# Attention over listed key blocks: tiles of 64 queries by three chunks of 128 keys, batch by batch over all heads

## The chip, the cores and the metric

The kernel runs on one core of one Trainium2 chip. The core has a tensor engine (PE; its weight loads are told apart as PEld), a vector engine (DVE), a scalar engine (ACT), GpSimd (POOL), a sync engine (SP) that mostly issues transfers, and 16 DMA engines that all queues share. Operands lie in on-chip memory of 128 partitions; the tensor engine writes its products into eight accumulation banks per partition.

The metric is the device time of one execution in microseconds. The kernel before took 692.69, 695.46 and 695.71 us in three runs: a median of 695.46 us.

## What is computed

Block-sparse attention, followed by a mixture of experts in which each token goes to one expert:

```python
# q, k, v: (4 batches, 8 heads, 768 positions, 64); blocks of 32, so 24 blocks
mask = |blk_i - blk_j| <= 1
mask |= (blk_i == 0) | (blk_j == 0) | (blk_i == 23) | (blk_j == 23)
for qb in range(24):
    for kb in sampled_blocks[qb]:            # 3 drawn blocks for each query block
        mask[qb*32:(qb+1)*32, kb*32:(kb+1)*32] = True
attn = softmax(where(mask, q @ k.T / 8, -1e9))
x = (attn @ v) with heads side by side       # (3072 tokens, 512)

logits = x @ w_gate                          # (3072, 8 experts)
expert = argmax(logits)
y = relu(x @ w1[expert]) @ w2[expert]        # 512 -> 1024 -> 512
return softmax(logits)[expert] * y
```

The drawn blocks are an input, so which keys a query sees is known only on the chip. An inner query block sees at most its own block and its two neighbours, the first and the last block, and three drawn ones. The first and the last query block see every key.

## The kernel before

Everything is float32; each float32 matmul shows in the trace as two weight loads and two matmuls.

**Attention** walks over 16 pairs `(b, pr)`: a batch and two heads, whose 64 dimensions fill the 128 partitions together. Each pair has two steps (`half`), for 384 of the 768 queries each, so 32 steps. `load` brings k, q and v of a pair on SP's queue, position p*6+c to partition p. `turn` transposes k and q by the tensor engine (12 transposes of 64x128) and ACT copies the result out. A step then makes six score units, one for each chunk c of 128 keys (`scores`): two products of 64x128 by 384 queries (line 244), one for each head, each on its half of the array's rows; an exp by ACT of the whole unit, 128x768 (line 249); and a product by DVE with a 0/1 mask (line 253). All keys are computed, and the mask removes those that are not listed. The mask for all 768x768 positions is built at the start (`make_mask`, `make_late`); the first step uses a penalty in the scores instead. `attend` multiplies the weights with v (line 265): for each chunk 12 products of 128 keys by 64 queries and 65 columns, the last column being ones, which gives the sum. Two such products stand side by side in the array, on 64 columns each.

After a step's last chunk, `divide` (DVE) takes sums, reciprocals and the product, and SP stores rows of x to DRAM in pieces of 512 bytes. One step later `turn_out` transposes x and ACT copies it, and `logits` multiplies it with the gate's weights. Logits are summed up over the four head pairs of a batch.

Scores, turned tiles and the mask's tables share a ring of three slots of accumulation memory (`ps_s`, two banks each); attention's products have one bank, x turned has one. The order of work on POOL, PE and DVE is the program's own, on ACT too in the loop of steps; the order on SP is left to the planner there.

**Routing and experts.** When three batches are done, phase A assigns their tokens to tiles of 128 tokens of one expert (`ranks`, `count`, `layout_a`, `slots_a`, `one_hots`, `tokens`), between attention steps of the last batch. Five such tiles are worked first; phase B places the rest while they run. Weights of an expert (2 MB for each of the two layers) are fetched by SP at an address read from a table; there are two buffers for each layer. Rows of x are gathered by POOL with an indirect DMA (`gather`), transposed, multiplied (`layer1`, line 815; `layer2`, line 829), and results are scattered to the output (`put`). Three larger and three small groups are worked among the tiles (`layers_u`, `layer1_s`, `layer2_s`).

At the end `judge` checks that all sums of exps and all logits lie in fixed bounds. If not, or if there are more tiles than foreseen, a switch runs more tiles or the whole of attention again with a maximum subtracted (`attention_again`).

Of the kernel before, what the change touches and what calls it, by code (L numbers as in the profile page):

```python
# [17 lines left out]
def kernel(  # L18
# [65 lines left out]
    ps_o = ctx.enter_context(tc.tile_pool(name="ps_o", bufs=1, space=PSUM))  # L84
    ps_x = ctx.enter_context(tc.tile_pool(name="ps_x", bufs=1, space=PSUM))
# [3 lines left out]
    def lend(to, **pools):  # L89
        to.close()  # L90
        for name, bufs in pools.items():
            upper[name] = to.enter_context(tc.tile_pool(name=name, bufs=bufs, space=PSUM, reuse_waits="tile"))

    lend(lent, ps_s=3)
    ld = ctx.enter_context(tc.tile_pool(name="ld", bufs=2))

    ea = mpool.tile([P, 8, NCH * P], F32, name="ea")

    def e_slot(n, half, c):
        return ea[:, ((2 * n + half) * NCH + c) % 8, :].rearrange("p (h q) -> p h q", h=2)  # L100

    HC = NCH // 2
    loaded, turned = {}, {}
    pairs = [(b, pr) for b in range(B) for pr in range(NPR)]
    NA = (B - 1) * NPR

    VW = D + 4
    values = [mpool.tile([P, 2, NCH, VW], F32, name=f"v_{j}") for j in range(3)]

    def load(b, pr):  # L110
        got = []
        for src, nm in ((k, "k_sb"), (q, "q_sb")):
            t = ld.tile([P, NCH, 2, D], F32, name=nm)
            for hh in range(2):
                nc.sync.dma_start(t[:, :, hh, :], src[b, 2 * pr + hh].rearrange("(p c) d -> p c d", p=P))
            got.append(t)
        t = values[pairs.index((b, pr)) % 3]
        for hh in range(2):
            nc.sync.dma_start(t[:, hh, :, :D], v[b, 2 * pr + hh].rearrange("(p c) d -> p c d", p=P))
        got.append(t)  # L120
        loaded[(b, pr)] = got


    oh = mpool.tile([P, NCH, P], BF16, name="oh")
    pen = mpool.tile([P, S], BF16, name="pen")
    assert NCH == 6
    mask = mpool.tile([P, NCH, S], BF16, name="mask")

    ones = mpool.tile([P, 1], F32, name="ones")

    sums = mpool.tile([P, 2 * B * NPR, 2 * HC], F32, name="sums")
    nc.vector.memset(ones[:], 1.0)

    def make_mask(pool):

        halves = bass.DRamTensorHandle(sampled_blocks.tensor.name, (2 * NB * NR,), I32)
# [823 lines left out]
    for which in range(2):  # L960
        turn(0, 0, which)
# [222 lines left out]
```

## Time and profile before

| | |
|---|---|
| three runs, median | 695.46 us (692.69 to 695.71) |
| profiled execution: its time / its span | 694.1 us / 692.4 us |
| first score product, first attention product | 8.65 us, 15.98 us |
| one step of attention | 9.69 us, constant from 31 to 263 us |
| last `divide` | 324.7 us |
| first expert matmul (line 815) | 325.9 us |
| from there to the end | 366.5 us |
| granted tensor clock, mean | 0.995 |

A line of the costliest groups names source line, engine, operation, what is written and read, the shape (a tensor operation's weights first, such as 128*64, then partitions x columns of the moving operand), and the count. Behind the first bar are busy microseconds and the mean nanoseconds of one; behind the second the engine's idle time ahead of them and what ended it. In the timeline a line starts with its start and its length. Matmuls overlap, so a mean of 223 ns for one says little; busy time over count is the pace.

### The profile page before, as it was taken

The page shows a single profiled execution, that of the slowest core. Times are in us where ns is not written, and L with a number is a line of the kernel's source. Part 1 is how long each engine was busy: PE and PEld are TensorE (multiplying, and loading weights), DVE is VectorE, ACT ScalarE, POOL GpSimd, SP SyncE. Part 2 cuts the span into 40 slices and gives each one's busy share as a digit, 9 for nine tenths or more (in the row PEclk, how much of TensorE's full clock was granted, in tenths as well). Part 3 has the DMA queues.
Part 4 walks back from the last instruction along what each step waited for, and adds up shares of the span by engine and source line. Part 5 has one row for each costly group of instructions (what it writes and reads, how often), then busy time and mean ns, then how long its engine had stood idle before and what let it go on. Part 6 is the DMA issues. An engine that isn't in the chain of part 4 may idle for free.

```text
span 692.4 us, 19727 instructions
## 1 busy us (share of the span) xinstructions
PE 671.0 (97%) x8586; PEld 511.7 (74%) x8586; DVE 340.5 (49%) x825; ACT 231.5 (33%) x393; POOL 66.2 (10%) x106
## 2 busy tenths in 40 slices
PE   8999999999999999998999999999999999999993
PEld 6777777777787777777867776696779778767861
DVE  6566766666666767885392059410254022702200
ACT  4555655566555664553211101112111111111110
POOL 4000000000000000003011221102120113010210
PEclk9999999999999999999999999999999999999998
DMA  9423443343323442853598999977996699989950
GB/s 190 102 64 86 94 93 86 81 94 93 77 60 78 93 94 50 332 204 88 171 317 303 307 340 383 343 278 259 402 397 235 239 387 393 358 274 390 396 173 18
DMA packets 135196, 145.78 MB, mean 211 GB/s; under 512 B 80995, under 2 KB 93283, under 8 KB 135076
## 3 DMA queue, kind: packets, MB, share of 16 engines
q1 hardware_dynamic: 130672, 130.15, 58.2%
q0 software_dynamic: 4368, 14.02, 5.3%
q8 instruction: 77, 1.26, 0.8%
q14 instruction: 43, 0.35, 0.2%
q10 hardware_dynamic: 36, 0.00, 0.0%
HBM read 131.47 MB, written 12.94 MB: 209 GB/s over the span
## 4 chain that ended last, share of the span: by engine, by line
PE 55%; issue 35%; POOL 4%; DVE 4%; POOLq 0%; another core or an unknown queue 0%; ACT 0%; DVEq 0%
PE op L265 20%; PE s L244 19%; PE hp L815 6%; PE zp L829 3%; PE tp L222 2%; PE xr L294 2%; POOL out_dram L844 2%; POOL xg L747 2%; PE xr L305 1%; PE idle L180 1%; DVE orB L677 1%; POOL ea L867 0%; POOL ea L912 0%; DVE tkB L697 0%; PE bm L195 0%
## 5 line engine op out<-in xcount | busy, mean ns | idle before, releaser
L253 DVE TENSOR_TENSOR ea<-ea,mask 128x768 f32<-128x768 f32 x186 | 164.3, 953 | 30.1 <-ACT ea L249 30.1
L265 PE MATMUL op<-v,ea 128*64 128x65 f32 x4608 | 148.4, 223 | 0.0
L815 PEld LDWEIGHTS hp<-xgT,w 128*128 128x128 f32 x1216 | 138.4, 192 | 8.9 <-issue 5.8
L265 PEld LDWEIGHTS op<-v,ea 128*64 128x64 f32 x4608 | 140.1, 138 | 5.9 <-DVE ea L253 4.4
L249 ACT ACTIVATE ea<-s 128x768 f32<-128x768 f32 x192 | 139.6, 851 | 13.8 <-PE s L244 10.8
L815 PE MATMUL hp<-xgT,w 128*128 128x128 f32 x1216 | 141.1, 276 | 2.7 <-ACT hT L822 1.4
L244 PE MATMUL s<-qT,kT 64*128 64x384 f32 x768 | 134.6, 495 | 0.8 <-DVE qT L228 0.8
L796 DVE STREAM_TRANSPOSE xgT<-xg 32x128 f32<-32x128 f32 x208 | 62.9, 303 | 128.9 <-PE hp L815 63.4
L829 PE MATMUL zp<-w,hT 128*128 128x512 f32 x256 | 112.7, 594 | 0.4 <-DMA w<-in_moe_w_dram 0.4
L244 PEld LDWEIGHTS s<-qT,kT 64*128 64x128 f32 x768 | 64.7, 186 | 51.2 <-ACT ea L249 32.5
L829 PEld LDWEIGHTS zp<-w,hT 128*128 128x128 f32 x256 | 47.6, 191 | 55.0 <-issue 54.3
L822 ACT ACTIVATE hT<-hp 128x512 f32<-128x512 f32 x36 | 21.5, 597 | 117.0 <-PE hp L815 98.6
L834 ACT ACTIVATE zo<-zp,xg 128x512 f32<-128x512 f32 x16 | 11.0, 687 | 101.3 <-PE zp L829 101.3
L922 DVE STREAM_TRANSPOSE ea<-ea 32x128 f32<-32x128 f32 x84 | 21.7, 285 | 30.1 <-DMA ea<-x_rows,gB 29.5
L747 POOL DMA_INDIRECT xg<-x_rows,gA x5 | 6.3, 1266 | 299.1 <-PE s L244 297.9
L230 ACT COPY kT<-tp 128x384 f32<-128x384 f32 x30 | 12.9, 482 | 63.4 <-PE tp L222 63.4
L230 ACT COPY qT<-tp 128x384 f32<-128x384 f32 x30 | 12.9, 483 | 61.4 <-PE tp L222 61.4
L844 POOL DMA_INDIRECT out_dram<-zo,sB x14 | 14.0, 1003 | 167.3 <-ACT zo L834 119.5
L313 DVE TENSOR_TENSOR lgn<-lgn,xr 128x24 f32<-128x24 f32 x24 | 4.3, 179 | 42.5 <-PE xr L305 42.5
L294 PEld LDWEIGHTS xr<-ident,xb 128*128 128x128 f32 x96 | 9.9, 140 | 16.9 <-DVE ea L253 15.3
L829 PE MATMUL hpu<-w,hT 128*128 128x512 f32 x48 | 21.1, 593 | 0.0
L933 PEld LDWEIGHTS hpu<-ea,w 128*128 128x128 f32 x96 | 15.2, 190 | 4.7 <-ACT zo L834 4.2
(279 smaller groups left out, 439.0 us busy)
## 6 DMA issues: line engine op xcount, KB each, us to landing
w<-in_moe_w_dram SPq DMA_DIRECT2D x50, 2048.0 KB, 10.8
k_sb<-in_k_dram SPq DMA_DIRECT2D x32, 192.0 KB, 4.2
q_sb<-in_q_dram SPq DMA_DIRECT2D x32, 192.0 KB, 3.3
v<-in_v_dram SPq DMA_DIRECT2D x32, 192.0 KB, 3.4
x_rows<-xb SPq DMA_DIRECT2D x16, 384.0 KB, 4.2
xg<-x_rows,gB POOLq DMA_INDIRECT x15
out_dram<-zo,sB POOLq DMA_INDIRECT x14
x_rows<-gw SPq DMA_DIRECT2D x4, 24.0 KB, 2.7
```

What stands on the lines that cost most here:

```text
L230: nc.scalar.copy(to[:, j], got[:, j])
L244: nc.tensor.matmul(s[:, hh, :CW], lhsT=kT[r, c * P : (c + 1) * P], rhs=qT[r, cols], start=True, stop=late)
L249: nc.scalar.activation(e, s[:, :, :CW], AF.Exp, scale=scale)
L253: nc.vector.tensor_tensor(e, e, m[:, None, :].to_broadcast([P, 2, CW]), op=ALU.mult)
L265: nc.tensor.matmul(op[j * D : (j + 1) * D, m, hh, : D + 1], lhsT=e[:, hh, m * P + j * D : m * P + (j + 1) * D], rhs=v_sb[:, hh, c, : D + 1 ...
L294: nc.tensor.transpose(xr[:, m * P : (m + 1) * P], xbs[n][:, half * HC + m, :], ident[:])
L796: nc.vector.transpose(xT[d, :, t], xg[t, :DM].rearrange("p (c q) -> p c q", c=DB)[:, :, d])
L815: nc.tensor.matmul(hp[:, m, :], lhsT=st[i]["w1"][:, c, fb * P : (fb + 1) * P], rhs=st[i]["xT"][:, c, :], start=(c == 0), stop=(c == DB - 1),)
L822: nc.scalar.activation(hT[:, g * (FB // 2) : (g + 1) * (FB // 2), :], hp[:], AF.Relu)
L829: nc.tensor.matmul(zp[:], lhsT=st[i]["hT"][:, fb, :], rhs=st[i]["w2"][:, fb, :], start=(fb == 0), stop=(fb == FB - 1),)
L844: ins = nc.gpsimd.indirect_dma_start(out=to[:, :], out_offset=bass.IndirectOffsetOnAxis(ap=at, axis=0), in_=rows, in_offset=None, bounds_c ...
L922: nc.vector.transpose(xT_u[d, :, j * P + tq * 32 : j * P + (tq + 1) * 32], xg_u[t, j, :DM].rearrange("p (c q) -> p c q", c=DB)[:, :, d],)
```

## The change

Attention is laid out anew; the experts' arithmetic stays.

**Tiles of queries.** The 22 inner query blocks make 11 tiles of 64 queries (two blocks each, tile t: blocks 2t+1 and 2t+2). Blocks 0 and 23 together are a twelfth. For each inner tile the keys are three chunks of 128: chunk 0 is the window, blocks 2t to 2t+3; chunk 1 is blocks 0 and 23 and two drawn blocks; chunk 2 is four drawn blocks. So 384 keys are computed for it instead of 768. A 0/1 mask per tile and chunk removes what a query does not see, drawn blocks that repeat or that the other chunks hold among it. The twelfth tile has all six chunks and no mask.

**Order.** The outermost loop is the batch, then a group g of two tiles (g = 5 first: the last inner tile and the end blocks; then 0 to 4), then two halves of two head pairs each: 48 steps. k and q of a whole batch, all heads, lie turned in one of two sets (`sets`); while a batch is worked, the next one's k and q are loaded (`fill_stage`), turned, and its v loaded.

**Scores.** A unit is again 128x768 and gets one exp and one mask product, but it is made of 24 products of 64 dimensions x 64 keys by 64 queries, one for each tile, chunk, head and half of a chunk, each on a 64x64 quarter of the array.

**Drawn blocks.** Keys: `place_keys` copies six blocks of 32 columns per tile, of all four head pairs at once (128x128), from the turned k to a buffer (`kr`), at addresses that ACT and DVE load into registers from a table; three on each, or all six on ACT for the last batch. Values: v of a batch is stored back to DRAM as rows of 520 numbers (all heads, each with its 1 for the sum; `keep_v`), and `fetch_values` gathers 128 such rows for each of chunks 1 and 2 with an indirect DMA on POOL, and the window that lies across two chunks with a plain one on SP.

**Around it.** x is stored as whole rows of 2048 bytes. Logits of 128 tokens are now summed over all heads in the accumulation memory. `turn_out` and phase A's small products use slots of the ring `ps_s`; attention's products have two banks. The order on ACT and SP is written out by hand too. The large mask and its tables go. The experts' buffers lie in memory that attention used (`room`, `around`, `kr`); two for each kind, as before. The twelfth tile of batch 0 is scored at the start, as each head pair arrives.

```diff
-    ps_o = ctx.enter_context(tc.tile_pool(name="ps_o", bufs=1, space=PSUM))
-    ps_x = ctx.enter_context(tc.tile_pool(name="ps_x", bufs=1, space=PSUM))
+    ps_o = ctx.enter_context(tc.tile_pool(name="ps_o", bufs=2, space=PSUM))
...
+    order = [GL] + list(range(GL))
+    VW = D + 1
+    VR = H * VW
+    NKR = 2 * NR * BLK
...
+    def load_v(b, hs=None):
+        for h in range(H) if hs is None else hs:
+            nc.sync.dma_start(sets[b][2][:, :, h * VW : h * VW + D], v[b, h].rearrange("(c p) d -> p c d", p=P))
+
+    def keep_v(b):
+        nc.sync.dma_start(v_d[b].rearrange("(c p) w -> p c w", p=P), sets[b][2])
...
+    def scores(items, m=None):
+
+        s = upper["ps_s"].tile([P, 2, 512], F32, name="s")
+        w = D * len(items)
+        for x, (keys, queries) in enumerate(items):
+            for hh in range(2):
+                r = slice(hh * D, (hh + 1) * D)
+                for j in range(2):
+                    nc.tensor.matmul(
+                        s[j * D : (j + 1) * D, hh, x * D : (x + 1) * D], lhsT=keys(r, j), rhs=queries(r), start=True, stop=True,
+                    )
+        e = ea[:, units[0] % 8, :].rearrange("p (h w) -> p h w", h=2)
+        units[0] += 1
+        nc.scalar.activation(e[:, :, :w], s[:, :, :w], AF.Exp, scale=scale)
+        return e
...
+    def unit(b, g, pr):
+        e = scores([(keys_of(b, g, pr, ti, ch), queries_of(b, g, pr, ti)) for ti in range(2) for ch in range(3)])
+        masked(e, g)
+        return e
...
+    def attend(b, g, pr, e):
+        for ch in range(3):
+            for hh in range(2):
+                for ti in range(2):
+                    x = 3 * ti + ch
+                    product(b, g, pr, ti, hh, e[:, hh, x * D : (x + 1) * D], values_of(b, g, ti, ch), ch == 2)
...
+    def fetch_values(b, g):
+        par = parity(b, g)
+        if g < GL:
+            row = D * (2 * g + 1)
+            nc.sync.dma_start(around[:, par, 0, :], v_d[b][row : row + P, :])
+        for ti, t in enumerate(tiles_of(g)):
+            for ch in range(2):
+                nc.gpsimd.indirect_dma_start(
+                    out=around[:, par, 1 + 2 * ti + ch, :], out_offset=None, in_=v_d[b][:, :],
+                    in_offset=bass.IndirectOffsetOnAxis(ap=rows_of[:, 2 * t + ch : 2 * t + ch + 1], axis=0),
+                )
+
+    def place_keys(b, g, ti, prs=slice(0, NPR), on_vector=NR):
+
+        t = tiles_of(g)[ti]
+        par = parity(b, g)
+        cut = 2 * NR - on_vector
+        for nm, a, z in (("Activation", 0, cut), ("DVE", cut, 2 * NR)):
+            if a == z:
+                continue
+            _, at = nc.values_load_multi_w_load_instructions(
+                from_k[0:1, NR + 2 * NR * t + a : NR + 2 * NR * t + z], engines=(getattr(mybir.EngineType, nm),),
+                min_val=0, max_val=S - BLK, skip_runtime_bounds_check_because="clamped on the chip to the blocks that there are",
+            )
+            for i, v_ in zip(range(a, z), at):
+                (nc.scalar.copy if nm == "Activation" else nc.vector.tensor_copy)(
+                    kr[:, par, ti, prs, i * BLK : (i + 1) * BLK], sets[b][0][:, prs, bass.ds(v_, BLK)],
+                )
...
+    steps = [(b, g, half) for b in range(B) for g in order for half in range(2)]
+    for i, (b, g, half) in enumerate(steps):
+        here = i % (2 * NG)
+        prs = (2 * half, 2 * half + 1)
+        nxt = steps[i + 2] if i + 2 < len(steps) else None
+
+        if g == GL:
+            if b > 0:
+                for pr in prs:
+                    es[("all", pr)] = unit_all(b, pr)
+            es[("two", half)] = unit_two(b, prs)
+        else:
+            for pr in prs:
+                es[pr] = unit(b, g, pr)
...
+        if nxt is not None:
+            b_, g_, half_ = nxt
+            if half_ < len(tiles_of(g_)):
+                place_keys(b_, g_, half_, on_vector=0 if b_ == B - 1 else NR)
...
+            if 2 <= here < 10:
+                turn(b + 1, (here - 2) // 2, here % 2)
+                if here < 6:
+                    fill_stage(b + 1, (here - 2) // 2 + 2, here % 2)
...
+        if i >= 3 and half == 1:
+            out_of = steps[i - 3][:2]
+            turn_out(*out_of)
+        if i > 0:
+            for b_, g_, pr, e_all, e in before:
+                if g_ == GL:
+                    attend_last(b_, pr, e_all, e)
+                else:
+                    attend(b_, g_, pr, e)
...
+        if out_of:
+            logits(*out_of)
...
+        if i > 0:
+            divide(*steps[i - 1])
+        if i >= 2 and half == 0 and nxt is not None:
+            fetch_values(*nxt[:2])
+        if b + 1 < B:
+            if here == 1:
+                load_v(b + 1)
+            if here == 4:
+                keep_v(b + 1)
```

## The prediction

> **What bounds the kernel now.** I read the shares and slices of the page first, then the costliest groups, then one attention step in the timeline, then the chain of waits.
>
> ```profile
> PE 671.0 (97%) x8586; PEld 511.7 (74%) x8586; DVE 340.5 (49%) x825; ACT 231.5 (33%) x393; POOL 66.2 (10%) x106
> ...
> DVE  6566766666666767885392059410254022702200
> ACT  4555655566555664553211101112111111111110
> ...
> DMA  9423443343323442853598999977996699989950
> ...
> L253 DVE TENSOR_TENSOR ea<-ea,mask 128x768 f32<-128x768 f32 x186 | 164.3, 953 | 30.1 <-ACT ea L249 30.1
> L265 PE MATMUL op<-v,ea 128*64 128x65 f32 x4608 | 148.4, 223 | 0.0
> ...
> L249 ACT ACTIVATE ea<-s 128x768 f32<-128x768 f32 x192 | 139.6, 851 | 13.8 <-PE s L244 10.8
> ...
> L244 PE MATMUL s<-qT,kT 64*128 64x384 f32 x768 | 134.6, 495 | 0.8 <-DVE qT L228 0.8
> ```
>
> Two stages meet at slice 18 or 19. Before it the DMA share is 0.3 to 0.4 and ACT and DVE work at about half; behind it the experts' weights keep the DMA engines at 0.9 and ACT and DVE are nearly idle. The change touches the first stage. In it the tensor engine never rests (210.0 of 210 us busy between 40 and 250), and one step repeats every 9.69 us:
>
> ```profile
> 103.57 3.58 PEld L265 LDWEIGHTS op<-v,ea 128*64 128x64 f32 x120 [0.17 <-DVE ea L253]
> ...
> 107.07 0.44 PEld L305 LDWEIGHTS xr<-wg,xo 128*64 128x64 f32 x12
> ...
> 108.27 0.45 PEld L222 LDWEIGHTS tp<-ident,k_sb 64*128 64x128 f32 x12
> ```
>
> The chain of waits shows 3.99 us of scores per step (six units of 0.665). With attention products at 3.58 us / 120 = 29.8 ns for a weight load and its matmul (a "pair"; every f32 product is two pairs), 144 of them take 4.3. Turn, transposes of x (0.55 for three) and logits fill the rest. The first expert matmul starts at 325.9; from there to the end are 366.5 us. I keep these 366.5: the change only moves the experts' small buffers into other memory, each still double.
>
> **What goes.** The stage has 192 score units of 128x768. The new one has 26 per batch (5 tile pairs times 4 head pairs, 2 units for the last tile, 4 for the two end blocks), so 104. Exps fall from 139.6 us of ACT to 104 x 139.6/192 = 75.6; mask products from 186 to 88, 164.3 to 77.7 us of DVE. A unit keeps 12 attention products, 24 x 29.8 ns = 0.72 us, except that the second half of the end blocks' chunks fills one column group alone (twice the price): 1.43 us per head pair there.
>
> **The score matmuls, the large unknown.** A unit was 4 pairs of 384 columns; it becomes 48 pairs of 64 columns, on four 64x64 quarters of the array. The trace has no such quarter. Nearest rows:
>
> ```profile
> L900 PE MATMUL zps<-w,ea 128*32 128x128 f32 x192 | 5.9, 274 | 0.0
> L883 PE MATMUL hps<-w,ea 128*32 128x256 f32 x96 | 5.8, 382 | 0.0
> L222 PE MATMUL tp<-ident,k_sb 64*128 64x64 f32 x192 | 9.4, 231 | 0.0
> ```
>
> Four column groups at once cost 31 ns a pair at 128 columns and 60 at 256. The difference is all stream, so 64 columns would cost 31 - 15 = 16. The other end: no row with short streams has a pair under 29.8 ns (L265), and if the tensor engine simply issues no faster, a quarter costs that too. I take 17 ns, since L900 is the row that also runs four parts: 0.82 us per unit. Ends 14.6 (0.70, no better than the stream of L244 allows) and 29.8 (1.43).
>
> A rule speaks against the change here. The Trainium skill, "TensorEngine Tiling (Array Packing)", section on instruction overhead, says that a matmul has some 60 cycles of overhead whatever its free size and that no tiling should be taken from a dimension that is already small; "TensorE: Matmul & The Clock Gate" (Part 1) puts the floor between starts at about 25 ns. By it a unit costs 1.2 us and the total below would be 690. In the trace the first four matmuls of L900 start 6 to 7 ns apart, so the floor may hold within one part of the array only.
>
> **What ACT gets.** place_keys copies six drawn blocks per tile, at addresses read into registers: three on ACT and three on DVE, in the last batch all six on ACT. Copy: L944's 128x160 takes 292 ns and 128x224 346, so 128x128 takes about 0.27. Register loads on ACT are in the trace once:
>
> ```profile
> L1088 ACTq TENSOR_LOAD <-xeU x3: 281/283/667, 352.7 to 354.3; - x3
> L1088 ACTq FUSED_REGOPS  x3: 147/163/176, 353.4 to 354.6; - x3
> ```
>
> So 0.28 to 0.59 each (0.59 is the pitch of the second and third, with checks that the change skips). I take 0.45. If the three registers of one call come in one load, all three cost 0.35; if checks remain in another form, 1.77. They stand in ACT's own order, between the second exp of a step and the copies; behind them wait the turn's copy (768 columns, 0.80, from 0.48 for 384), the copy of x for the logits (0.59, as L805's 128x512), and for that the logits on PE.
>
> **One step.** A step is half a tile pair: two units, a turn (8 of 12 steps), attention of the step before; in odd steps x is transposed and the logits are done.
> - Even step, set by PE: 2 x 0.82 + turn 0.38 + 2 x 0.72 + about 0.5 for four changes of shape (0.1 to 0.15 idle each in the timeline) = 4.0.
> - Odd step, set by ACT: second unit done at 1.64, its exp (851 ns) at 2.5; loads from 1.64 to 3.0; copies 3.8; turn's copy 4.6; x's copy 5.2; then 16 pairs of logits 0.48 and hand-overs 0.2: 5.9. PE idles about 1.3 us of it.
> - DVE, per step: two mask products 1.9, three copies 0.25 each, loads half hidden behind the masks 0.5, divide 0.8: 3.95, so it follows.
>
> Batch of 12 steps: end blocks 4.5 + 6.7 (three units each, 2.5; attention of 2.9 in the second, x and logits 0.9), steps 2 and 3 5.2 + 5.9, three pairs of 9.9, last pair without turns 3.7 + 5.1: **61 us**. Last batch: no turns, but six loads and six copies on ACT. Odd step: loads to 4.3, copies 5.9, x 6.5, logits 7.2; even step 5.1. Four such pairs 49.2, last pair 8.8, end blocks 12, and 3.7 for phase A's tables (before, three of its steps were 1.0 to 1.3 longer): **74 us**.
>
> **Start.** First products need only two loads, as before. But batch 0's values must land, go out to memory as whole rows and come back by list: SP issues 8 stage and 8 value loads (0.7 each); 18,432 packets of 256 B at 22 ns over 16 engines are 25 us with the late stage loads; the write follows, 768 rows of 2 KB at 84 ns (half of the 169 ns of the 4160 B packets) over 16 engines, 4 us; then one gather, 3 to 4 us. The end blocks of batch 0 are done at about **38** us; cover for PE till then (turns, four units, their attention) is some 13 us. The rest of batch 0 is 48.
>
> **Sum.** 38 + 48 + 61 + 61 + 74 = 282 instead of 325.9. Plus 366.5 is a span of 648.5, plus 1.7 around the span (694.1 - 692.4) 650; the profiled execution lies 1.4 under the median 695.46, so **652**.
>
> **Costed at nothing, and the cover.** Value gathers: 4 per tile pair, on POOL, which had nothing to do before 316.
>
> ```profile
> L747 POOL DMA_INDIRECT xg<-x_rows,gA x5 | 6.3, 1266 | 299.1 <-PE s L244 297.9
> ```
>
> At a pitch of 1.6 us and landing 3 us after the last issue, 9.5 us; they are issued after the attention of one step and used three steps on, some 14 us. Without that cover, each microsecond late costs 20 over the run. DMA share: per batch 18,432 packets at 18.4 ns, 3,456 value rows and 1,536 rows of keep_v and x at 84 to 88, over 16 engines: 21 + 18 + 8 = 47 us of 61, against 0.37 before. It fits, with bursts in each batch's first half. SP's row stores and window loads queue behind waits for stage buffers, whose turns come first anyway. The 2 KB rows of x replace 512 B pieces, no cost.
>
> The Trainium skill, "Runtime: NRT & Kernel Launch" (Instruction fetch mechanics), gives some 200 ns per loaded register, under the 283 of L1088; by it the odd step is 0.75 shorter at most and the total about 626.
>
> **Rivals.**
> 1. *Small pairs issue no faster than L265's.* At 29.8 ns a unit takes 1.43, 0.61 more; 100 units of the loop are 61 us: **713, slower**. One nanosecond per pair is 4.8 us; it passes the old time at about 26 ns. For it: no short-stream row is below 29. Against: L900 and its dense starts.
> 2. *One load brings all registers, or they hide behind the exps.* Odd steps fall to 5.2 (15 of them in three batches, -11 in all), the last batch's pairs to 9.3 (-15): **626**.
> 3. *Values or drawn keys come late.* If the bursts hold each gather up by 1 us more than its cover: 20 tile pairs, **672**. Against: 4.5 us of slack.
> 4. *Nothing is saved since the check at the end takes the second path* (dense attention again). Sums of exps over the same keys pass the same bounds; under 1%.
>
> **Chances.** Forecast 0.52, rival 1 0.21, rival 2 0.14, rival 3 and its like 0.13 (mostly still faster). Anything beyond 0.5% (3.5 us) can be told from no change here. Faster 0.74, same 0.05, slower 0.21. Range: from rival 2 with 14.6 ns pairs (626 - 11 = 615) up to a pair of 28 ns (652 + 53 = 705).
>
> **What will show it.** Score pairs near 17 ns in a burst, 48 per 0.82 us; first expert matmul near 284 us; odd steps longer than even ones, with logits waiting for ACT's copy of x; ACT's register loads as gaps of 0.6 us or less after the second exp; last batch slowest. Wrong if PE is again busy without a gap while steps exceed 6.4 us (rival 1), if attention waits for a DMA (rival 3), or if the tail is no longer 366 us.

## The result and the profile after

The changed kernel took **720.50 us** (median of 4 runs, 718.73 to 721.48) and the kernel before 694.08 (692.68 to 695.71): a ratio of 1.0377, interval [1.034, 1.0414]. It is slower by 3.8%; the forecast was 652, and its range ended at 705. The profiled execution took 720.11 with a span of 718.4. First the shares and slices of its page, to be read against those shown of before.

```profile
PE 606.9 (84%) x10680; PEld 505.6 (70%) x10680; DVE 275.6 (38%) x874; ACT 208.4 (29%) x431; POOL 157.3 (22%) x203
...
PE   3578887677787978716999999999998999999994
...
DVE  0435453445445544724358035720227001902200
ACT  1135553455445654613311110111110211111110
...
PEclk8588899999999899967999999999999999999998
DMA  9699848876698634794379899996999399979960
...
q8 instruction: 97, 1.59, 0.9%
```

PE's slices and its clock in the kernel before:

```profile
PE   8999999999999999998999999999999999999993
PEclk9999999999999999999999999999999999999998
```

DVE, ACT and PE all have less work, as the change intends (PE 671.0 to 606.9 us, DVE 340.5 to 275.6). But in the first 19 slices PE is now mostly at 0.6 to 0.8 instead of full (0.3 at the start, 0.1 in slice 18), its clock is not full either, and the DMA share has gone from 0.3 or 0.4 to mostly 0.6 and more. The first expert matmul (now L1041) starts at 351.9 us, forecast 282, before 325.9. From there to the end it is 366.5 us, as before to a tenth. So the whole miss, 69.9 us, lies in attention. The costliest groups of that stage:

```profile
L485 POOL DMA_INDIRECT around<-v_rows,rows_of x88 | 91.5, 1040 | 219.5 <-PE op L355 184.2
L310 ACT ACTIVATE ea<-s 128x768 f32<-128x768 f32 x104 | 81.9, 810 | 165.2 <-PE s L305 163.3
...
L355 PE MATMUL op<-around,ea 128*64 128x65 f32 x1728 | 85.8, 238 | 22.5 <-DMA around<-v_rows 15.7
...
L318 DVE TENSOR_TENSOR ea<-ea,mask 128x768 f32<-128x768 f32 x80 | 74.6, 955 | 47.6 <-ACT ea L310 46.4
```

ACT was idle 165.2 us ahead of its exps, 163.3 of them for PE's scores: PE still sets the pace, with ACT and DVE waiting. Yet PE has gaps. Its waits, us in total, times, longest:

```profile
PE s L305 <- issue: 27.9, 20, 3.2
PE s L305 <- DVE room L154: 19.2, 4, 15.7
PE op L355 <- DMA around<-v_rows: 15.7, 1, 15.7
PE op L355 <- issue: 15.3, 13, 3.1
PE xr L449 <- ACT xo L433: 10.8, 14, 2.0
```

The largest part, "issue", is time in which PE waited for nothing that the profile shows. One of these gaps in the timeline, in the middle of a run of attention products:

```profile
156.01 0.33 PE L355 MATMUL op<-around,ea 128*64 128x65 f32 x4
159.46 0.62 PE L355 MATMUL op<-around,ea 128*64 128x65 f32 x13 [3.12 <-issue]
```

No operand is waited for by this view, and the same line goes on 3.12 us later. Counting the records of TensorE's two queues (TensorE is PE; the queues are those of its matmuls and its weight loads) in order of start, 30 of the 45 gaps over 0.4 us (from 25 us to the first expert matmul) fall on the same number, 193 of each 256; each of these 30 (45.4 us together) has a packet of 16,384 bytes on the queue of kind "instruction" (q8 above) that ended 1.20 to 1.62 us ahead of the gap's end. If such a packet holds 256 instructions, they are 64 bytes each; the reading is that TensorE has run to the end of the program that it had been brought, and the third session tests it. A block of 256 takes a median of 3.5 us where the DMA share is under 0.35 in it (14 blocks after 60 us) and 5.4 where it is over 0.75 (30 blocks), with mean gaps of 0.4 and 1.1 us at the border. The kernel before has 3 gaps over 0.4 us in the same stretch (2.8 us), none at such a border: its longer matmuls use up some 39 records per us, these up to 117 (48 pairs in 0.82 us).

Other waits are from two places. The four DVE waits (19.2 us) are the start: the first score matmul comes at 23.5 us (8.7 before), since POOL's memset of the ones columns (L262), and behind it the tables, stand after batch 0's value loads. And 15.7 us at 311 are the last batch's values. SP's queue at that time:

```profile
302.38 0.38 SPq L1005 DMA_DIRECT2D room<-in_moe_w_dram  x1
302.86 14.03 SPq L421 DMA_DIRECT2D x_rows<-xb  x1
316.99 0.47 SPq L482 DMA_DIRECT2D around<-v_rows  x1
```

A row store that otherwise issues in 0.34 us took 14.03 behind four weight transfers of 2 MB, and the window of values (L482) stood behind it.

Behind some of the gaps the granted clock is 0.5 for stretches of 3.4 us or a multiple. Between first score and first expert matmul these are 72.7 us; before there were none. After 40 us there are 11 such stretches, and each begins within 1.6 us of the end of a gap of 1.2 to 3.3 us; but 12 gaps of 1.2 to 3.1 us, that at 156 us among them, are followed by none.

### The profile page after: what moved, and what is told of

It reads as the page before. It is cut to its first block, busy times and chain, and to the rows that moved or that the text cites. A ratio compares the mean times of both kernels' runs of the same rounds, so it can differ in the third digit from the quotient of the medians.

```text
span 718.4 us, 24445 instructions
## 1 busy us (share of the span) xinstructions
PE 606.9 (84%) x10680; PEld 505.6 (70%) x10680; DVE 275.6 (38%) x874; ACT 208.4 (29%) x431; POOL 157.3 (22%) x203
## 5 line engine op out<-in xcount | busy, mean ns | idle before, releaser
L1041 PEld LDWEIGHTS hp<-around,room 128*128 128x128 f32 x1216 | 138.3, 192 | 7.3 <-issue 5.1
L1041 PE MATMUL hp<-around,room 128*128 128x128 f32 x1216 | 140.8, 276 | 1.4 <-ACT kr L1048 1.4
L485 POOL DMA_INDIRECT around<-v_rows,rows_of x88 | 91.5, 1040 | 219.5 <-PE op L355 184.2
L310 ACT ACTIVATE ea<-s 128x768 f32<-128x768 f32 x104 | 81.9, 810 | 165.2 <-PE s L305 163.3
L1022 DVE STREAM_TRANSPOSE around<-xg 32x128 f32<-32x128 f32 x208 | 62.9, 303 | 131.0 <-DMA xg<-x_rows,gB 87.4
L1055 PE MATMUL zp<-room,kr 128*128 128x512 f32 x256 | 112.7, 594 | 0.2 <-DMA room<-in_moe_w_dram 0.2
L355 PE MATMUL op<-around,ea 128*64 128x65 f32 x1728 | 85.8, 238 | 22.5 <-DMA around<-v_rows 15.7
L355 PEld LDWEIGHTS op<-around,ea 128*64 128x64 f32 x1728 | 77.8, 152 | 24.8 <-DMA around<-v_rows 15.9
L318 DVE TENSOR_TENSOR ea<-ea,mask 128x768 f32<-128x768 f32 x80 | 74.6, 955 | 47.6 <-ACT ea L310 46.4
L1055 PEld LDWEIGHTS zp<-room,kr 128*128 128x128 f32 x256 | 47.5, 190 | 54.9 <-issue 54.4
L305 PE MATMUL s<-room 64*64 64x64 f32 x1088 | 40.4, 244 | 22.3 <-DVE room L154 19.2
```

Source lines behind the costliest of these rows:

```text
L305: nc.tensor.matmul(s[j * D : (j + 1) * D, hh, x * D : (x + 1) * D], lhsT=keys(r, j), rhs=queries(r), start=True, stop=True,)
L310: nc.scalar.activation(e[:, :, :w], s[:, :, :w], AF.Exp, scale=scale)
L318: nc.vector.tensor_tensor(e, e, m[:, None, :].to_broadcast([P, 2, w]), op=ALU.mult)
L355: nc.tensor.matmul(op[ti * D : (ti + 1) * D, pr % 2, hh, : D + 1], lhsT=e, rhs=values[:, (2 * pr + hh) * VW : (2 * pr + hh + 1) * VW], sta ...
L485: nc.gpsimd.indirect_dma_start(out=around[:, par, 1 + 2 * ti + ch, :], out_offset=None, in_=v_d[b][:, :], in_offset=bass.IndirectOffsetOnA ...
L1022: nc.vector.transpose(xT[d, :, t], xg[t, :DM].rearrange("p (c q) -> p c q", c=DB)[:, :, d])
```

## The experiments

Kernels of one session (a "call" in the expectations) ran one after the other on one chip, beside runs of the kernel before, which took 693.3 to 694.1 us in every session. Times are medians.

### First session: one cost each

**Ones columns first** (e1): the memsets ahead of batch 0's loads.

```
+    for two in (sets[0][2], sets[1][2]):
+        nc.gpsimd.memset(two.rearrange("p c (h w) -> p c h w", w=VW)[:, :, :, D], 1.0)
     load_v(0)
-    for two in (sets[0][2], sets[1][2]):
-        nc.gpsimd.memset(two.rearrange("p c (h w) -> p c h w", w=VW)[:, :, :, D], 1.0)
```

> Edit: the two memsets of the ones columns of v are issued ahead of batch 0's v loads instead of behind them. In the changed kernel the first of them waits on POOL until 17.5 us, the tables' chain behind it holds DVE until 22.4, and PE idles from 7.7 to 23.5. Theory (a false order at the start): PE's first scores come at about 8.5 us, the write of v goes out at some 19 us instead of 28, attention ends 9 to 13 us earlier: 708 to 712 us. Rival (the loads of v set the start anyway): under 4 us are gained, 717 us or more.

**Last batch's windows on POOL's queue** (e2).

```
-            nc.sync.dma_start(around[:, par, 0, :], v_d[b][row : row + P, :])
+            (nc.gpsimd if b == B - 1 else nc.sync).dma_start(around[:, par, 0, :], v_d[b][row : row + P, :])
```

> Edit: in the last batch the window's values are fetched through POOL's queue instead of SP's. In the changed kernel that fetch is issued at 317 us, behind a store that waits 14 us on SP behind 8 MB of expert weights, and PE idles 15.7 us. Theory (the queue): the stall falls under 4 us and the half clock after it goes: 700 to 706 us. Rival (the DMA engines themselves are full until the weights are in, whichever queue asks): the stall stays above 10 us, 715 us or more.

**Wide weights** (e3): 64x128 key weights where the keys lie side by side.

```
+                if keys.whole:
+                    nc.tensor.matmul(s[:, hh, x * D : (x + 1) * D], lhsT=keys.whole(r), rhs=queries(r), start=True, stop=True)
-                for j in range(2):
+                for j in range(0 if keys.whole else 2):
```

> Edit: score products of chunks 0 and 2, and of all chunks of the end blocks, take 128 keys as weights (64x128) instead of two times 64; same arithmetic, same transfers, some 3,600 of 17,000 tensor instructions of attention fewer. Theory F (instructions arrive in blocks of 256, and a block takes 4.7 us on average to come): 14 blocks fewer, 66 us less for fetching, against up to 0.35 us more stream per unit, 36 us in all, that partly lies in what were stalls: 670 to 700 us. Rival R (nothing is short of instructions; the gaps are hand-overs between engines): the longer stream is simply added, 735 to 755 us.

**Without loads** (e4).

```
         if b + 1 < B:
-            if here == 0:
-                for pr in range(2):
-                    for which in range(2):
-                        fill_stage(b + 1, pr, which)
             if 2 <= here < 10:
                 turn(b + 1, (here - 2) // 2, here % 2)
-                if here < 6:
-                    fill_stage(b + 1, (here - 2) // 2 + 2, here % 2)
...
-            if here == 1:
+            if here == 1 and b == 0:
                 load_v(b + 1)
```

> Edit: the loads of k and q for batches 1 to 3 and of v for batches 2 and 3 are left out, so those batches work on old data; all instructions of PE, ACT, DVE and POOL stay. Theory F: a block of instructions comes in 3.4 to 4.0 us instead of 4.7 when the DMA engines are quiet; 62 blocks, 40 to 70 us less: 650 to 680 us, and stalls of PE above 0.5 us that begin at a block's border fall from about 30 to under 10. Rival R (PE's own pace of short pairs, or ACT's chain): unchanged within 5 us.

Measured: 777.32, 775.82, 816.44 and 819.92 us, ratios to before of 1.1209 [1.1174, 1.1243], 1.1195 [1.1142, 1.1249], 1.1744 [1.1703, 1.1785] and 1.1796 [1.1755, 1.1837]. None was expected. All are 55 us and more above the unedited kernel's first runs, though e1 leaves the order of instructions on PE, ACT and DVE as it was. In their traces TensorE is slow above all at one place: while POOL issues the gathers (L485) it starts some 20 to 27 records per us in most groups of four, against 37 to 74 in the changed kernel's first trace. So the next session began with a control.

### Second session: the control, and the gathers taken away

> The changed kernel itself once more, unedited. In the profiles of the four experiments before, TensorE starts 20 to 25 records per us while POOL issues the gathers (4 per step, some 4.8 us), in the changed kernel's first profile 57 to 73. If that difference came with the edits: 717 to 723 us again. If it belongs to the chip on which those four ran, and not to the edits, and this chip is like it: 765 to 785 us, with 20 to 25 records per us under the gathers.

**No gathers** (e6).

```
-            for ch in range(2):
+            for ch in range(2 if b == 0 and g in (GL, 0, 1) else 0):
                 nc.gpsimd.indirect_dma_start(
```

> Leaves out the gathers of the drawn value rows after the third step of batch 0 (76 of 88), so later steps use old rows. Theory G (TensorE is starved while POOL issues gathers): against the unedited kernel of the same call, 20 steps lose 3 to 4 us each where the records fall to 22 per us, so 60 to 75 us less than it; where they stay at 65 per us, 5 to 20 us less (only the transfers' load goes). Theory F (only the fetch of TensorE's own program and the start and window waits cost time): within 15 us of the unedited kernel in both cases.

**Gathers on SP** (e7).

```
+            _, at = nc.values_load_multi_w_load_instructions(
+                from_k[0:1, NR + 2 * NR * t : NR + 2 * NR * (t + 1)], engines=(mybir.EngineType.SP,),
...
+            for i, v_ in enumerate([0, S - BLK] + list(at)):
+                p = i % 4 * BLK
+                nc.sync.dma_start(around[p : p + BLK, par, 1 + 2 * ti + i // 4, :], v_d[b][bass.ds(v_, BLK) if i > 1 else slice(v_, v_ + BLK), :])
-            for ch in range(2):
-                nc.gpsimd.indirect_dma_start(
```

> The gathers leave POOL: SP loads six block numbers per tile of queries and issues eight transfers of 32 rows per tile (two for the end blocks' rows, six at register addresses). By the page SP's issues take 0.36 us and a load of six registers 1.3, so 16 x 0.36 + 2 x 1.3 = 8.4 us of SP per step of some 12. Theory G: as without gathers, 50 to 75 us below the unedited kernel if that one starves, 0 to 15 below if not. Rival (SP's queue becomes the bound, with the window and row stores behind it): 10 to 40 us above the unedited kernel, with TensorE waiting on DMA for around.

**Both first edits** (e8): e1 and e2 together.

> Both earlier edits at once: the ones columns set ahead of batch 0's value loads, and the last batch's windows on POOL's queue. If the start (first score matmul 23.4 us) and the window wait (15.7 us, then 20 us at half clock) are costs as the first profile shows them: 20 to 35 us below the unedited kernel of this call. If the two edits themselves slow the rest, as the four runs before could also be read: 40 us or more above it.

Measured: the unedited kernel 786.91 us here (ratio 1.133 [1.1295, 1.1364]). It is 66 us above its own first runs, so that difference doesn't come with the edits. Without gathers 729.30 (1.0496 [1.0457, 1.0534]), and there the changed data gave the experts more tiles, so the stage tells more: first expert matmul at 337.1 us against 424.2, **87 us** for 78 gathers (10 of 88 are left, not 12 as the expectation has it; theory G, 60 to 75 us, is nearly met by the time as a whole, 58 us less; theory F alone allowed 15). The windows of the trace show it. First the unedited kernel beside e6 and e8, under four gathers, then the same four in a later session (c2, below); columns are the stretch, its length, busy time and instructions of PE, PEld, DVE, ACT, POOL, granted clock, DMA share, GB/s.

```profile
61.75:66.59 4.84, 2.46 (x62) 1.61 (x62) 1.17 (x6) 0.20 (x1) 3.92 (x4) 1.00 0.82 213
```

```profile
57.76:62.60 4.84, 4.48 (x160) 3.90 (x160) 3.26 (x10) 3.73 (x8) 3.92 (x4) 1.00 0.92 232
```

Same four gathers, same 3.92 us of POOL, same full clock: 62 matmuls in one, 160 in the other. Inside, the slow kind looks like this:

```profile
192.16 0.34 PE L305 MATMUL s<-other,kr 64*64 64x64 f32 x4 [0.45 <-issue]
...
192.91 0.27 PE L305 MATMUL s<-other,kr 64*64 64x64 f32 x2 [0.40 <-issue]
...
193.62 0.35 PE L305 MATMUL s<-other 64*64 64x64 f32 x6 [0.39 <-issue]
```

Four or five pairs, then a pause, every 0.7 us, with nothing named that PE waits for. The wide weights of e3 fall to the same 24 records per us under the gathers, though each carries twice the keys: that points at the supply of instructions and not at the array. It isn't the fetch in blocks of 256 that sets this pace: of the 32 blocks in the control's batches 1 and 2, only 12 begin within 1.65 us of their packet's end (27 of 32 in the first trace).

e7 took 816.89 us, 30 above the control: PE no longer starves (136 matmuls in a stretch of 4.84 us), but it waits 113.5 us for `around`, the buffer of gathered values, since SP needed 137 us for 330 issues and 65 for 42 register loads (1.54 each for six registers) in the first 424 us. The rival held. e8 took 767.84, 19 below, just short of the 20 to 35 expected; the window edit had moved the wait: PE waits 12.5 us for the routing's one-hots, since DVE's divide ahead of them waits 13.7 us for a buffer whose row store still stands behind the weights.

Against this control the first session, which starved too, can be read, though on another chip (the two starving controls, c1 and c3, end attention at 424.2 and 425.3 us). Start: e1's attention ends at 408.2 us, 16 earlier. Window: e2's at 409.4, 15 earlier. Loads: e4's at 416.1, only 8 earlier, where 40 to 70 were expected; that fits the 12 of 32 above, since a faster fetch can't help much where the fetch isn't what PE waits for. Wide weights: e3's at 452.3, 28 later, since in unbroken runs of 16 a wide pair took a median of 52 ns between starts and a narrow one 13, and two narrow ones do its work.

### Third session: which part of a gather, and what the borders are

> The changed kernel unedited, as the mark of this call. 717 to 723 us with 57 to 73 TensorE records per us under the gathers, as in its first profile, or 780 to 795 us with 20 to 27, as in the control of the call before. No other value is expected: the two differ by what happens under the gathers alone.

**Half of the gathers on SP** (f9), with e1 and e2.

```
+            if b < B - 1:
+                if (b, par, ti) not in globals_in:
+                    globals_in.add((b, par, ti))
+                    for i, row in enumerate((0, S - BLK)):
+                        nc.sync.dma_start(around[i * BLK : (i + 1) * BLK, par, 1 + 2 * ti, :], v_d[b][row : row + BLK, :])
+                _, at = nc.values_load_multi_w_load_instructions(
+                    from_k[0:1, NR + 2 * NR * t : NR + 2 * NR * t + 2], engines=(mybir.EngineType.SP,),
...
+                for i, v_ in enumerate(at):
+                    nc.sync.dma_start(around[D + i * BLK : D + (i + 1) * BLK, par, 1 + 2 * ti, :], v_d[b][bass.ds(v_, BLK), :])
-            for ch in range(2):
+            for ch in range(1 if b < B - 1 else 0, 2):
```

> Both earlier edits (ones columns first, last windows on POOL's queue) and half of POOL's gathers gone in batches 0 to 2: SP brings the two drawn blocks of the chunk that holds the end blocks, at register addresses, and the end blocks' own rows once per batch and buffer. 33 of 88 gathers fall away; without 76 of them attention was 87 us shorter in the control's call, so 33 are worth about 38. Theory G: 19 (both edits, as measured) + 38 = 57 us below the unedited kernel if that one starves (725 to 740 us), 20 to 35 below if not (685 to 700). Rival (SP's queue): SP's added 66 transfers of 0.42 us and 33 register loads of some 0.5 us delay windows and stores: 0 to 25 us below.

**POOL kept busy** (f10).

```
             for ch in range(2):
+                if not (b == 0 and g in (GL, 0, 1)):
+                    for _ in range(5):
+                        nc.gpsimd.memset(around[:, par, 1 + 2 * ti + ch, :].rearrange("p (h w) -> p h w", w=VW)[:, :, D], 1.0)
+                    continue
```

> Leaves out the gathers after the third step of batch 0, and puts in the place of each five memsets of POOL on the ones column of the same rows (0.2 us each), which keep the old values; so the same 1 us of POOL at the same place with the same wait, but no descriptors and no transfer. Theory D (the making of the descriptors is what starves TensorE): within 10 us of the run without gathers (f11), 60 records or more per us under the memsets. Rival P (any work of POOL at that place does it, by its port to SBUF): 20 to 30 records per us under them and 50 us or more above f11.

**Program shifted** (f11): e6 and 64 more warm-up transposes.

```
-        for c in range(22):
+        for c in range(22 + 64):
             nc.tensor.transpose(idle[:, 0, :P], ident[:], ident[:])
```

> Leaves out the same gathers, and adds 64 warm-up transposes on TensorE ahead of the first work, while it waits for batch 0's data: 128 more records, every later instruction 128 places further on. Theory F (TensorE runs out of its own program at the border of a fetched block of 256 instructions): the gaps stay at record numbers near 193 of each 256, 20 or more of them, each with a fetch packet of 16,384 bytes in it, at places of the program 128 records earlier than without the shift; the time stays within 10 us of the same kernel without the shift (724 to 738 us). Rival (the gaps belong to places of the program, to waits that the profile doesn't show): they move to numbers near 65 of 256.

Measured: the unedited kernel 723.15 (1.0412 [1.0377, 1.0448]), as in its first runs, with 39 to 74 records per us under groups of four gathers (31 where PE waits for the window). Its attention ends at 357.7 us. f9 711.60, f10 718.24, f11 721.85. The last two have the experts' additional tiles in them (tails of 393 and 394 us instead of 365); their attention ends at 324.9 and 327.6.

- f10's and f11's attention ends within 3 us of each other, and PE starts 56 to 117 records per us under the memsets. In the third session nothing starved, and 20 memsets took 2.9 us where four gathers take 4.8, so f10 shows only that such work of POOL costs nothing here; whether memsets would starve PE in the other kind of session wasn't seen.
- f11: 25 of 38 gaps still at number 193, all with their packet, though every instruction now stands 128 places further on. The gaps belong to the count and not to a place of the program: theory F holds in this. (The time, 721.85, is 2 us under the range expected, which came from a starving session.)
- Without the 78 gathers attention is 30 us shorter even in a session without starving.
- f9 gains 11.5 us, against 20 to 35 expected; the rival, SP's queue, had 0 to 25. Its SP queue shows the same block as before, and PE waits 13.1 us for the routing.

### Fourth session: does the sum close

> The changed kernel unedited, as the mark of this call: 717 to 726 us with 40 to 75 TensorE records per us under the gathers, or 780 to 795 us with 20 to 27.

**Weights spread** (g1): with e1, the last batch's four weight transfers one at a time.

```
-            for i_ in range(2):
-                fetch(i_, 1)
-                fetch(i_, 2)
+        if i in (3, 5, 7, 9):
+            fetch((i - 3) // 4, 1 + (i - 3) // 2 % 2)
```

> Ones columns set ahead of batch 0's value loads, and the four weight transfers of 2 MB that the last batch issues at once now issued two half-steps apart. Theory Q (the window's wait of 15 us, and the 20 us at half clock behind it, come from the stores and windows that stand in SP's queue behind 8 MB): no wait for around above 3 us, no SP store over 4 us, and against the unedited kernel 15 us from the start and 15 to 25 from the window: 685 to 698 us where that one takes 720. Rival (the routing of the last batch or the first expert's weights come later, and the time is given back): 8 to 16 us below the unedited kernel, with TensorE waiting for orA or for the weights.

**With half of the gathers on SP** (g2): g1 and the edit of f9.

> As g1, with half of POOL's gathers of batches 0 to 2 on SP as in f9. 76 gathers less were worth 30 us of attention on the chip of the call before, so 33 less 13, minus what SP's work costs: 5 to 13 us below g1, 675 to 690 us where the unedited kernel takes 720, under the kernel before the change. Rival (SP's queue gives it back): within 4 us of g1.

**The floor** (g3): g1 with the edits of e4 and e6.

> Leaves out the gathers after the third step of batch 0, the loads of k and q for batches 1 to 3 and of v for 2 and 3; with the two edits of g1. What is left in attention is the program itself, with little transfer traffic. If the forecast's step times hold and only these costs were missed, the first expert matmul comes at 282 + 10 = 285 to 297 us. Theory F (TensorE's program fetch costs time even on an idle memory: 3.3 us and more for each of some 65 blocks that the pairs alone would run through in 2.5 to 3): 295 to 310 us, with 15 or more gaps at record numbers near 193 of 256, shorter than with the loads. The time is not compared: the changed data give the experts another number of tiles.

Measured: a starving session again, the unedited kernel 789.89. g1 768.27 (21.6 below, just short of the 22 or more that theory Q asked for): no wait for around is left among PE's longer waits, none for the routing, and no row store of SP takes over 0.6 us, so taking the block away does what moving it didn't. g2 728.24, another 40.0 for 33 gathers, where 5 to 13 were expected: that price came from a session without starving. g3's first expert matmul comes at 306.2 us, with 17 gaps at number 193 (21.6 us), as theory F had it (295 to 310, 15 gaps or more). The last three batches of three kernels, as windows from one batch's first exp to the next's: the changed kernel's first trace, f11 (no gathers), g3 (no gathers, no loads).

```profile
110.00:188.00 78.00, 59.26 (x2115) 54.29 (x2104) 37.12 (x104) 37.15 (x76) 22.61 (x22) 0.96 0.74 199
188.00:265.00 77.00, 61.42 (x2093) 56.14 (x2089) 36.08 (x101) 38.01 (x78) 22.30 (x22) 0.91 0.74 197
265.00:347.00 82.00, 52.58 (x1892) 49.13 (x1887) 38.97 (x109) 34.51 (x91) 25.96 (x24) 0.83 0.63 216
```

```profile
109.70:178.80 69.10, 57.06 (x2105) 52.18 (x2101) 35.96 (x103) 36.72 (x76) 0.00 (x0) 0.98 0.52 133
178.80:248.60 69.80, 58.16 (x2104) 53.41 (x2098) 35.47 (x100) 37.49 (x79) 0.00 (x0) 0.95 0.51 130
248.60:323.00 74.40, 52.59 (x1891) 48.71 (x1882) 38.61 (x110) 34.78 (x91) 4.05 (x4) 0.84 0.48 167
```

```profile
104.40:166.70 62.30, 55.85 (x2101) 50.91 (x2094) 35.84 (x104) 36.78 (x76) 0.00 (x0) 1.00 0.25 77
166.70:231.30 64.60, 56.44 (x2105) 51.77 (x2101) 35.19 (x101) 37.33 (x79) 0.00 (x0) 0.97 0.23 75
231.30:301.30 70.00, 55.49 (x1892) 50.63 (x1881) 38.89 (x109) 34.96 (x92) 3.95 (x4) 0.90 0.52 177
```

The busy times of PE, DVE and ACT hardly differ. What falls in batches 1 and 2 is the DMA share, 0.74, 0.52, 0.25, and the batch with it: 78, 69, 62 us in batch 1. In the last batch the share does not fall from f11 to g3 (0.48, 0.52), since the experts' weights come in it, and g3 has these weights spread besides. The forecast was 61, 61 and 74.

### Fifth session: fewer gathers

**Half in all batches** (h1): g2 with `b < B - 1` left off. **Most** (h2): for the first tile of each step SP brings all six drawn blocks.

```
-                    from_k[0:1, NR + 2 * NR * t : NR + 2 * NR * t + 2], engines=(mybir.EngineType.SP,),
+                    from_k[0:1, NR + 2 * NR * t : NR + 2 * NR * t + (6 if ti == 0 else 2)], engines=(mybir.EngineType.SP,),
...
-            for ch in range(1, 2):
+            for ch in range(2 if ti == 0 else 1, 2):
```

> As g2, with half of the gathers on SP in the last batch too (44 of 88 left on POOL). On a chip where TensorE falls to 20 to 30 records per us under the gathers: 33 fewer gathers were worth 40 us from g1 to g2, so 11 more are worth 13: 712 to 720 us. On the other kind (60 records or more): g2's edits there are worth 15 + 12 for start and window and 13 for the gathers, so 678 to 700 us. Rival (in the last batch SP's queue stands behind the weights, 2 MB at a time): no gain over g2 or a loss, with waits for around above 4 us.

> As h1, and for the first tile of each step SP brings all six drawn blocks, so POOL keeps 20 of 88 gathers (one a step). Theory G: 24 gathers fewer, 25 to 30 us below h1 on the kind of chip that starves (683 to 695 us), 5 to 9 below on the other (670 to 692). Rival (SP's queue becomes the bound, as when it did all): per step SP needs two register loads (1.5 and 0.5 us), eight transfers of 0.42 us and its loads and stores, some 9 of 12 us; TensorE then waits for around, and the time is 0 to 40 us above h1.

Measured: h1 716.24 (1.0323 [1.0268, 1.0378]), h2 736.56 (1.0603 [1.0555, 1.065]). Under h1's gathers PE starts mostly 65 to 97 records per us, so this is the other kind of session (the unedited kernel was not run in it; g2, which differs in the last batch alone, had 18 to 46 under most of its gathers). By that its expectation of 678 to 700 was missed; that 716 lies in the 712 to 720 of the starving kind then says nothing for it. Its waits:

```profile
PE s L306 <- issue: 26.1, 25, 2.8
PE op L356 <- issue: 16.3, 11, 2.3
PE op L356 <- DMA around<-v_rows: 8.1, 5, 2.5
```

The long window wait and the late start are gone, and 34 gaps at number 193 have come to 50.2 us (49.8 in c2). Batches 1 and 2 take 79.9 and 77.9 us, in c2 75.7 and 79.6: rows brought by SP are the same traffic, and here, where PE doesn't starve, they save nothing. h2, 20 above h1, waits 30.9 us for around: SP's queue again, as its rival had it.

No version that does all the work beat the kernel before (g3, at 703.47, leaves out loads and gathers); nearest came f9, 711.60 us, at a ratio of 1.026 [1.0199, 1.032].

## Why the prediction was wrong

The step that failed is **"Costed at nothing, and the cover"**. It asked whether the values arrive in time and whether the bytes fit. They do: PE's one long wait for values is for a window on SP's queue, not for gathered rows, and the cover of 14 us was enough, so rival 3 as stated didn't happen, though its sign, attention waiting for a DMA, showed once. But both have another customer. TensorE's own program comes through the same DMA engines in blocks of 16 KB, and 128 pairs of 17 ns use up a block of 256 in some 2.2 us. "47 us of 61" was read as room left over; for PE it was a slower fetch. Priced by the runs, per batch: gathers 7 to 10 us (batches 1 to 3 of c2 against f11: 75.7, 79.6, 83.4 to 69.1, 69.8, 74.4), loads of the next batch another 4 to 7 (f11 against g3 of another session, in the last batch with the weights spread as well). Of these the border gaps are shown to be the fetch (f11). For the rest the packets speak. In batches 1 and 2 no block of these three traces begins sooner than 1.20 us after its packet's end, and most begin within 1.65 us of it, with a gap over 0.4 us or without:

| batches 1 and 2 | first trace | f11 | g3 |
|---|---|---|---|
| blocks that begin within 1.65 us of their packet's end | 27 of 32 | 24 of 31 | 26 of 32 |
| packet's start after the block before began, mean | 2.14 us | 1.44 us | 1.23 us |
| one block, mean | 4.72 us | 4.25 us | 3.88 us |

So PE follows its program's packets in most blocks, and with more transfers the packets start later, in sum by about as much as the blocks grow. What holds a packet back wasn't seen. In sessions where PE starves under the gathers' issue, which is another cost, the 78 gathers cost 87 us instead of 30.

Point by point:

- **Score pair 17 ns: right.** 48 pairs in one burst at full clock:

```profile
36.23 0.82 PEld L305 LDWEIGHTS s<-room 64*64 64x64 f32 x48 [1.25 <-ACT room L154]
```

  0.82 us, as forecast; the median of the 104 units is 0.84. The rule on matmul overhead that spoke against it (25 ns, the Trainium skill, "TensorE: Matmul & The Clock Gate", Part 1) is not borne out by this burst, and rival 1, the forecast's way to "slower", fell: the kernel became slower by another way.
- **Three register loads of 0.45, 1.35 in all: too dear.** One instruction brings all of them: 0.69 us at least, 0.80 in the median of ACT's 44 (0.70 for the 34 that bring three, 1.34 for the 10 that bring six), 3.07 at most. That lay between the forecast and rival 2's 0.35.
- **Batches of 61, 61 and 74: right for the work, wrong for its surroundings.** Without gathers and loads they took 62.3, 64.6 and 70.0.
- **Odd steps set by ACT:** in kind, PE waits for ACT's copy of x 14 times, 10.8 us together; next to the fetch it is small.
- **Start, 38 us:** the first two divides of batch 0 came at 53.0 and 58.3. The step overlooked that the ones columns' memset stands behind the value loads; without that the first scores come 15 us earlier (8.5 in f9), but batch 0 ends only 5.7 earlier than c2's (107.2 against 112.9), and POOL's first gather then waits for the values' write until 30.3 us. What holds batch 0 (some 24 of the 69.9 us) wasn't taken apart; in g3 it still ends at 104.4 us, 18 after the forecast.
- **SP's stores and windows, put at "no cost": wrong in the last batch.** 14.03 us of queue, 15.7 of PE. In the kernel before a row store among the last batch's weights took 7.54 us instead of some 0.6, but nobody waited for it.
- **Tail 366.5: right.**

So batch 0 gave 24 us of the miss (110.2 against 86), batches 1 and 2 33 (154.9 against 122), the last batch 13 (to the first expert matmul at 351.9: 86.8 against 74).

A page bears on the step that failed. The Trainium skill, "Runtime: NRT & Kernel Launch", Instruction fetch mechanics, says that an engine's program is refilled in blocks of 16 KB and that this is mostly hidden. The blocks are in this trace; hidden they are not, with 45.4 us of gaps at their borders.

What stays open: why the unedited kernel takes 720 to 723 us in two sessions and 787 to 790 in two others. All kernels of a session show the same kind under whatever gathers they have, and the kernel before is left alone. It isn't a fixed property of a chip: the chip of the second session, where PE starved, also ran the fifth, where it didn't by the records under the gathers.

## What to carry to other kernels

When a change trades few long matmuls for many short ones, divide the number of instructions by 256 and ask what brings each block: here, below some 3.5 us per block, TensorE ran at the pace of its program's fetch, and the transfers that the change added slowed it, even those that landed in time. A DMA share that fits need not be free for such a stretch. And run the unedited kernel again beside the first experiments: without that control, four runs here would have been read as four bad edits.

## What was not expected of the hardware

- While POOL issues indirect gathers (0.95 us each, pitch 1.25), TensorE can fall to 20 to 27 records per us at full clock, for 64x64 and 64x128 weights alike; in other sessions the same gathers left it at 37 to 74.
- Some gaps of 1 to 3 us were followed by half clock, others by none: 72.7 us of it in attention's first trace, 169.8 and 172.8 in the starving controls. What the half clock alone costs wasn't tried.
- A 64x128 weight pair of 64 columns took more than two 64x64 pairs on quarters of the array: 52 ns between starts against 13, median of unbroken runs of 16 (e3).
